# Cumulative sums on 128 partitions and a first q/k pair by heads, in an attention and MLP kernel

## The chip, the cores and the metric

The kernel runs on one core of a Trainium2 chip. A core has five engines that run side by side, each through its own list of instructions in order: TensorE (matrix products), VectorE, ScalarE and GpSimd (work on elements), and SyncE (starts transfers). Sixteen DMA engines move data between the main memory and the on-chip memory SBUF. TensorE writes to a small second memory, PSUM, from which VectorE and ScalarE copy the results. Engines wait for each other through semaphores.

The metric is the device time of one execution in microseconds (us), as the median of several runs. The profiled execution is a run of its own, and its span is a little shorter than its device time, since it counts from the first to the last instruction.

## The reference

Eight batches of eight heads, 576 tokens, head size 64. Each head has q, k, v, and a row s of one number per token.

```python
def attention(q, k, v, s):                       # (8, 8, 576, 64), s: (8, 8, 576)
    scores = (1 / sqrt(64)) * q @ k.T
    cum = cumsum(maximum(s, 0), axis=-1)
    bias = -(cum[:, :, :, None] - cum[:, :, None, :])
    scores = where(causal, -1e9, scores + minimum(bias, 0))
    attn = softmax(scores)                       # over the keys
    return attn @ v

x = attention(...)  # heads side by side: (8, 576, 512)
xn = layernorm(x) * g_ln
out = x + maximum(xn @ w_ch1, 0) @ w_ch2         # 512 -> 2048 -> 512
```

The cumulative sum never falls, so below the diagonal the bias is never positive, and the minimum with 0 changes nothing there. The bias is a term of the query minus a term of the key. The kernel therefore adds it in the scores' own matrix product, by four more rows (64 to 67) beside the 64 of the head size. On the key side they hold the cumulative sum as three bf16 numbers (high, middle and low part, whose sum is nearly exact) and a row of constants; on the query side they hold the high part and constants.

## The kernel before

The kernel is in bf16 after its loads. At its start it does three things at once: it makes the cumulative sums of all 64 heads in float32, it brings q and k of the first heads into the layout that the products need (head size on partitions, tokens along the row), and it loads v. Two heads make a pair. A pair is loaded with six neighbouring tokens to a partition (96 partitions), transposed by TensorE into PSUM, and evacuated from there into the tile kq by VectorE and ScalarE.

```python
QT = 6                      # tokens to a partition
QP = S // QT                # 96 partitions

def ld_pair(kind, g):                            # float32, by SyncE
    tmp = stage.tile([P, 2, QT * D], F32, name="pairtmp", tag="st")
    nc.sync.dma_start(out=tmp[0:QP], in_=pair_src(kind, g))

def ld_cast(kind, g):                            # to bf16 on the way, by GpSimd
    ready[kind, g] = pair_tile(kind)             # from a pool of four buffers
    nc.gpsimd.dma_start(out=ready[kind, g][0:QP], in_=pair_src(kind, g))

def tr_kind(kind, g):                            # six transposes
    ...
    for t in range(QT):
        nc.tensor.transpose(tr[:, t * QP : (t + 1) * QP], src..., ident[0:QP, 0:QP])

def evac_pair(kind, g, engs):                    # two copies, each of both heads
    ...

def keep_warm(n):                                # matmuls on zeros: filler
    for _ in range(n):
        nc.tensor.matmul(w, lhsT=zeros[:, 0:P], rhs=zeros, start=True, stop=True)
```

The start, in the order of the program (every engine takes its own instructions out of it in this order):

```python
nc.sync.dma_start(out=c_in, in_=s.rearrange("b h s -> (b h) s"))    # 64 rows of 576
ld_pair("k", 0)
ld_pair("q", 0)
...                                              # constants are set
keep_warm(12)
...
ld_cast_pair(1); ld_cast_pair(2)
for t in range(NT): ld_cast_v(0, t)              # five tiles of v of batch 0
ld_cast_pair(3); ld_w1(0)
...
nc.vector.tensor_scalar(out=c_in, in0=c_in, ...)                    # relu, times 8
nc.vector.tensor_tensor_scan(out=c_sc, data0=c_one, data1=c_in, ...)   # cumulative sum
cast_pair("k", 0, "act")
cast_pair("q", 0, "act")
nc.vector.tensor_copy(out=c_hi, in_=c_sc)                           # three bf16 parts
nc.vector.tensor_tensor(out=c_in, in0=c_sc, in1=c_hi, op=ALU.subtract)
nc.vector.tensor_copy(out=c_mid, in_=c_in)
nc.vector.tensor_tensor(out=c_lo, in0=c_in, in1=c_mid, op=ALU.subtract)
aug(0, nc.sync, h0=1)         # rows 64 to 67 of heads 1 to 3, SBUF to SBUF by DMA
...
nc.tensor.matmul(ba, lhsT=pick[:, 3, :], rhs=ones[:, 0:512], start=True, stop=False)
tr_kind("k", 0)
keep_warm(2)
tr_kind("q", 0)
nc.tensor.matmul(bq, lhsT=pick[:, 0, :], rhs=c_hi[:, 0:512], ...)   # rows 64 to 67 of head 0
for j, src in enumerate((c_hi, c_mid, c_lo)):
    nc.tensor.matmul(ba, lhsT=pick[:, j, :], rhs=src[:, 0:512], ...)
    ...                                          # one filler between
...                                              # bb: the same for the last 64 tokens
evac_pair("k", 0, ("act", "act"))
nc.scalar.copy(out=kq[0][D : D + 1, 1, 0, 0:512], in_=bq[32:33])
evac_pair("q", 0, ("dve", "act"))
nc.vector.tensor_copy(out=kq[0][D:KA, 0, 0, 0:512], in_=ba[0:4])
nc.vector.tensor_copy(out=kq[0][D:KA, 0, 0, 512:S], in_=bb[0:4, 0:TL])
nc.vector.tensor_copy(out=kq[0][D : D + 1, 1, 0, 512:S], in_=bb[32:33, 0:TL])
keep_warm(5)
```

Then the heads follow, n = 0 to 63. For the first eight:

```python
scores(b, h)                  # sa, sb, sc: products into PSUM; then exp by ScalarE
if h in (1, 3, 5, 6): scores_d(b, h // 2)
if h in (0, 2, 4):            # pairs 1, 2, 3
    qk_pair(h // 2 + 1, ("dve", "dve"), ("act", "dve" if h < 4 else "act"))
...
if n % 2 == 1 or n == 0: keep_warm(2)
if n > 1: pv_next()           # product with v of an earlier head (pot), VectorE divides by the sum
```

After head 8 TensorE also has the two products of the MLP (ph and py) in a queue, and units of that queue fill it up between the heads until the end.

Of the kernel before, what the change touches and what calls it, by code (L numbers as in the profile page):

```python
# [19 lines left out]
def kernel(  # L20
# [11 lines left out]
    nc = tc.nc  # L32
    B, H, S, D = q.shape
# [9 lines left out]
    BH = B * H  # L43
# [7 lines left out]
    NR = 4  # L51
    QT = 6
    QP = S // QT

    const = ctx.enter_context(tc.tile_pool(name="const", bufs=1))
    stage = ctx.enter_context(tc.tile_pool(name="stage", bufs=6))
# [29 lines left out]
    cT = const.tile([P, NT, 2, BH, 4], BF16, name="cT")  # L86
    xm = [const.tile([P, Dm], F32, name=f"xm{i}") for i in range(4)]
    xTm = const.tile([P, KD, 512], BF16, name="xTm")
    c3 = const.tile([BH, 3, S], BF16, name="c3")
    c_hi, c_mid, c_lo = (c3[:, j, :] for j in range(3))  # L90
    zeros = const.tile([P, 512], BF16, name="zeros")
    ones = const.tile([BH, S], BF16, name="ones")
    minus = const.tile([1, S], BF16, name="minus")
# [12 lines left out]
    ready = {}  # L106


    def pair_src(kind, g):
        src = k if kind == "k" else q  # L110
        b, j = g // 4, g % 4
        return src[b, 2 * j : 2 * j + 2].rearrange("h (p t) d -> p h (t d)", t=QT)

    def pair_tile(kind):
        return pairs.tile([P, 2, QT * D], BF16, name=kind + "p", tag=kind + "p")

    def ld_pair(kind, g):
        tmp = stage.tile([P, 2, QT * D], F32, name="pairtmp", tag="st")
        nc.sync.dma_start(out=tmp[0:QP], in_=pair_src(kind, g))
        loaded[kind, g] = tmp  # L120

    def cast_pair(kind, g, eng):
        ready[kind, g] = pair_tile(kind)
        copy_on(eng, ready[kind, g][0:QP], loaded.pop((kind, g))[0:QP])

    def ld_cast(kind, g):
        ready[kind, g] = pair_tile(kind)
        nc.gpsimd.dma_start(out=ready[kind, g][0:QP], in_=pair_src(kind, g))

    def ld_cast_pair(g):  # L130
        ld_cast("k", g)
# [112 lines left out]
        tr_kind("k", g)  # L244
        tr_kind("q", g)

    def tr_kind(kind, g):
        src = ready.pop((kind, g))
        if g < 5:
            tr = ps_m.tile([P, S], BF16, name="trqk", tag="m")  # L250
        else:
            tr = ps_t.tile([P, S], BF16, name="trqk", tag="tr")
        for t in range(QT):

            nc.tensor.transpose(
                tr[:, t * QP : (t + 1) * QP],
                src[0:QP].rearrange("p h c -> p (h c)")[:, t * P : (t + 1) * P],
                ident[0:QP, 0:QP],
            )
        trs[kind, g] = tr  # L260

    def evac_pair(kind, g, engs):
        tr = trs.pop((kind, g))
        hh = (g % 2) * 2
        dst = kq[(g // 2) % 2][0:D, "kq".index(kind), hh : hh + 2, 0:S].rearrange(
            "d u (p r w) -> d u p r w", r=QT // 2, w=2
        )
        for w in range(2):
            copy_on(
                engs[w],  # L270
                dst[:, :, :, :, w],
                tr[w * D : (w + 1) * D, :].rearrange("d (u r p) -> d u p r", u=2, p=QP),
            )

    def qk_pair(g, k_engs, q_engs):
# [289 lines left out]
    def keep_warm(n):  # L565
# [2 lines left out]
            nc.tensor.matmul(w, lhsT=zeros[:, 0:P], rhs=zeros, start=True, stop=True)  # L568


    c_in, c_sc, c_one, warm = (
        yop.tile([P, S], F32, name="c_in", tag="yo")[0:BH],
        yop.tile([P, S], F32, name="c_sc", tag="yo")[0:BH],
        yop.tile([P, S], F32, name="c_one", tag="yo")[0:BH],
        small.tile([P, 2], F32, name="warm", tag="warm", bufs=1),
    )
    nc.sync.dma_start(out=c_in, in_=s.rearrange("b h s -> (b h) s"))
    ld_pair("k", 0)
    ld_pair("q", 0)

    ONE2 = 1.0019378662109375
    NEG2 = -1.0058441162109375
    nc.vector.memset(zeros.bitcast(F32), 0.0)
    nc.vector.memset(warm, 0.0)
    nc.scalar.activation(out=warm[:, 1:2], in_=warm[:, 0:1], func=ACT.Exp)
    keep_warm(12)
    nc.vector.memset(c_one, 1.0)
    nc.vector.memset(pick.rearrange("p j m -> p (j m)").bitcast(F32), 0.0)
    for j in range(3):
# [31 lines left out]
    for t in range(NT):  # L621
        ld_cast_v(0, t)
    ld_cast_pair(3)
    ld_w1(0)
    v_edges(1)
    nc.vector.tensor_scalar(
        out=c_in, in0=c_in, scalar1=0.0, scalar2=1.0 / scale, op0=ALU.max, op1=ALU.mult
    )
    nc.vector.tensor_tensor_scan(
        out=c_sc, data0=c_one, data1=c_in, initial=0.0, op0=ALU.mult, op1=ALU.add  # L630
    )
    cast_pair("k", 0, "act")
    cast_pair("q", 0, "act")
    nc.vector.tensor_copy(out=c_hi, in_=c_sc)
    nc.vector.tensor_tensor(out=c_in, in0=c_sc, in1=c_hi, op=ALU.subtract)
    nc.vector.tensor_copy(out=c_mid, in_=c_in)
    nc.vector.tensor_tensor(out=c_lo, in0=c_in, in1=c_mid, op=ALU.subtract)
    aug(0, nc.sync, h0=1)
    constant_rows(1)
    aug(1, nc.sync)  # L640
# [3 lines left out]
    bb = ps_s.tile([P, 512], F32, name="bb", tag="s")  # L644
    bq = ps_s.tile([P, 512], F32, name="bq", tag="s")
    nc.tensor.matmul(ba, lhsT=pick[:, 3, :], rhs=ones[:, 0:512], start=True, stop=False)
    tr_kind("k", 0)
    keep_warm(2)
    tr_kind("q", 0)
    nc.tensor.matmul(bq, lhsT=pick[:, 0, :], rhs=c_hi[:, 0:512], start=True, stop=True)  # L650
    for j, src in enumerate((c_hi, c_mid, c_lo)):
        nc.tensor.matmul(
# [4 lines left out]
    for j, src in ((3, ones), (0, c_hi), (1, c_mid), (2, c_lo)):  # L657
        nc.tensor.matmul(
            bb[:, 0:TL], lhsT=pick[:, j, :], rhs=src[:, 512:S], start=(j == 3), stop=(j == 2)
        )  # L660
# [213 lines left out]
```

The softmax here doesn't subtract the row's maximum and nothing guards it: scores larger than these inputs give would overflow.

## Time and profile before

| what | value |
|---|---|
| device time, median of 3 runs | 367.0 us (366.61 to 367.05) |
| span of the profiled execution | 366.8 us |
| TensorE busy | 355.0 us, 97% |
| VectorE busy | 202.9 us, 55% |
| ScalarE busy | 191.3 us, 52% |
| GpSimd busy | 164.9 us, 45% |
| moved by DMA | 52.17 MB, 142 GB/s on average |

In the lines of the profile, PE is TensorE, PEld its loading of weights, DVE VectorE, ACT ScalarE, POOL GpSimd and SP SyncE. L12 is line 12 of the kernel. An output and an input are given as `out<-in` by their tiles' names. A busy share is an average over the whole span, and a start of ten or twenty microseconds can look quite different from the rest; so the views that matter here are those that keep the order of time: the chain of waits (followed back from the last instruction, at each step to what released it) and the timelines of single engines. A long start of a matmul after the one in front of it doesn't say by itself what TensorE waited for; the filler matmuls are work too in the profile's eyes.

### The profile page before, as it was taken

How to read it: one execution, taken by the hardware profiler on the slowest of the kernel's cores; microseconds unless marked ns; L12 is line 12 of the kernel's file. 1: busy time of each engine (PE TensorE's matmuls, PEld its weight loads, DVE VectorE, ACT ScalarE, POOL GpSimd, SP SyncE). 2: the span in 40 equal slices, each digit the busy share in tenths (PEclk: the TensorE clock that was granted, in tenths of full speed). 3: DMA queues.
4: the chain of work that ended last, by engine and by line, in shares of the span. 5: the costliest groups of instructions: out<-in, count | busy, mean ns of one | idle time of the engine just before them, and what ended most of it. 6: DMA issues, size and time to landing. Idle time of an engine off the chain costs nothing.

```text
span 366.8 us, 8315 instructions
## 1 busy us (share of the span) xinstructions
PE 355.0 (97%) x3017; PEld 197.1 (54%) x3067; DVE 202.9 (55%) x535; ACT 191.3 (52%) x367; POOL 164.9 (45%) x447
## 2 busy tenths in 40 slices
PE   8998999999999999999999999999999999999995
PEld 3677555565555555555455555555555554444444
DVE  7697789684357554944384547743675483112211
ACT  5895988467732673367534753476337522501410
POOL 8854468667633656344675563554852101000000
PEclk9999999999999999999999999999999999999999
DMA  8999999999965999599979986798830011011013
GB/s 144 162 195 178 202 211 193 163 240 176 183 146 141 206 199 181 104 215 163 188 176 213 194 183 140 189 191 182 174 102 2 0 59 57 1 58 59 0 31 86
DMA packets 156653, 52.17 MB, mean 142 GB/s; under 512 B 143641, under 2 KB 151940, under 8 KB 156612
## 3 DMA queue, kind: packets, MB, share of 16 engines
q1 hardware_dynamic: 138868, 43.08, 55.5%
q0 software_dynamic: 17344, 8.03, 18.9%
q8 instruction: 24, 0.39, 0.5%
q10 hardware_dynamic: 400, 0.52, 0.4%
q14 instruction: 17, 0.14, 0.2%
HBM read 37.11 MB, written 9.44 MB: 127 GB/s over the span
## 4 chain that ended last, share of the span: by engine, by line
PE 72%; DVE 7%; DMA 6%; SPq 4%; POOL 4%; issue 3%; ACT 3%; POOLq 0%; ACTq 0%
PE py L515 26%; PE ph L497 25%; PE pot L389 6%; SPq L164 3%; PE sc L312 3%; PE sa L312 3%; PE sb L312 3%; DMA rowtmp<-in_q_dram 2%; PE idle L568 2%; DMA vtmp<-in_v_dram 2%; DVE xn L451 2%; PE trx L484 2%; DVE stats L423 1%; POOL er L331 1%; ACT er L323 1%
## 5 line engine op out<-in xcount | busy, mean ns | idle before, releaser
L515 PE MATMUL py<-w_bf,hT 128*128 128x512 bf16 (+1 forms) x565 | 132.1, 373 | 1.6 <-DVE yo L524 0.4
L497 PE MATMUL ph<-xT,w_bf 128*128 128x512 bf16 x478 | 116.4, 379 | 1.1 <-DVE yo L524 0.2
L507 ACT ACTIVATE hT<-ph 128x512 bf16<-128x512 f32 x102 | 61.0, 598 | 64.4 <-PE ph L497 64.4
L515 PEld LDWEIGHTS <-hT 128*128 128x128 bf16 x592 | 53.5, 98 | 49.1 <-issue 0.9
L497 PEld LDWEIGHTS <-w_bf 128*128 128x128 bf16 x560 | 50.1, 97 | 51.3 <-issue 2.9
L323 ACT ACTIVATE er<-sa 128x512 bf16<-128x512 f32 x64 | 38.2, 597 | 70.9 <-PE sa L312 50.1
L331 POOL TENSOR_SCALAR_AFFINE_SELECT er<-er 128x128 bf16<-128x128 bf16 x216 | 59.7, 300 | 22.5 <-ACT er L323 22.3
L505 DVE TENSOR_SCALAR hT<-ph 128x512 bf16<-128x512 f32 x38 | 26.3, 692 | 56.7 <-PE ph L497 49.0
L176 POOL CAST rows<-rowtmp 128x512 bf16<-128x512 f32 (+1 forms) x55 | 33.5, 609 | 50.7 <-DMA rowtmp<-in_q_dram 46.0
L312 PEld LDWEIGHTS <-kq 68*128 68x128 bf16 x452 | 33.4, 97 | 27.4 <-issue 1.7
L389 PEld LDWEIGHTS <-er 128*128 128x128 bf16 x960 | 37.5, 98 | 14.9 <-issue 0.7
L389 PE MATMUL pot<-v_bf,er 128*128 128x65 bf16 x960 | 40.2, 193 | 0.5 <-PE sd L355 0.3
L397 DVE RECIPROCAL rinv<-pot 128x5 f32<-128x5 f32 x64 | 12.3, 192 | 49.2 <-PE pot L389 48.9
L323 ACT ACTIVATE er<-sc 128x512 bf16<-128x512 f32 x64 | 39.2, 612 | 0.0
L323 ACT ACTIVATE er<-sb 128x512 bf16<-128x512 f32 x64 | 38.4, 599 | 0.3 <-PE sb L312 0.2
L524 DVE SCALAR_TENSOR_TENSOR yo<-py,rstd,xb 128x512 f32<-128x512 f32 x32 | 23.9, 748 | 26.2 <-PE py L515 19.7
L399 DVE TENSOR_TENSOR xb<-pot,rinv 128x256 f32<-128x256 f32 x64 | 27.2, 425 | 2.2
L102 POOL CAST v_bf<-vtmp 128x512 bf16<-128x512 f32 (+1 forms) x30 | 18.5, 617 | 19.6 <-DMA vtmp<-in_v_dram 19.5
L439 POOL TENSOR_TENSOR rstd<-rstd,mhalf 128x4 f32<-128x4 f32 (+1 forms) x8 | 8.8, 1095 | 38.0 <-DVE rstd L438 37.9
L312 PE MATMUL sc<-kq 68*128 68x256 bf16 (+1 forms) x216 | 25.3, 229 | 0.3
L423 DVE BATCH_NORM_STATS2 stats<-xb 128x6 f32<-128x128 f32 (+2 forms) x100 | 25.3, 313 | 0.4
L312 PE MATMUL sb<-kq 68*128 68x64 bf16 (+1 forms) x172 | 24.5, 244 | 0.9 <-DMA kq<-rows 0.6
(101 smaller groups left out, 322.1 us busy)
## 6 DMA issues: line engine op xcount, KB each, us to landing
out_dram<-yo SPq DMA_DIRECT2D x32, 256.0 KB
vtmp<-in_v_dram SPq DMA_DIRECT2D x24, 256.0 KB
rowtmp<-in_k_dram SPq DMA_DIRECT2D x44, 128.0 KB
rowtmp<-in_q_dram SPq DMA_DIRECT2D x44, 128.0 KB
w_bf<-in_moe_w_ch_dram POOLq DMA_DIRECT2D x8, 512.0 KB, 10.7
kp<-in_k_dram POOLq DMA_DIRECT2D x9, 144.0 KB, 6.8
qp<-in_q_dram POOLq DMA_DIRECT2D x9, 144.0 KB, 7.0
v_bf<-in_v_dram POOLq DMA_DIRECT2D x8, 128.0 KB, 8.1
```

The costliest lines, as they stand in the source:

```text
L176: nc.gpsimd.tensor_copy(out=r[0:pn, :, :, 0:D], in_=loaded.pop(("rows", gam, t))[0:pn])
L312: nc.tensor.matmul(a[:, c + a0 - q0 : c + a1 - q0], lhsT=k_cols(b, h, kb), rhs=cols, start=True, stop=not (pe_mask and diag),)
L323: nc.scalar.activation(out=e[:, o : o + 512], in_=a, func=ACT.Exp, scale=scale)
L331: nc.gpsimd.affine_select(out=e[:, o : o + P], in_=e[:, o : o + P], compare_op=ALU.is_ge, fill=0.0, base=0, pattern=[[1, P]], channel_mult ...
L389: nc.tensor.matmul(pot[:, t, :], lhsT=e[:, o : o + P], rhs=vv[:, kb, h, :], start=(kb == 0), stop=(kb == last),)
L399: nc.vector.tensor_tensor(out=xb[b][:, :, hs], in0=pot[:, 0:NF, 0:D], in1=rinv[:, 0:NF].unsqueeze(2).to_broadcast([P, NF, D]), op=ALU.mult,)
L423: nc.vector.bn_stats(out=st[b][:, t, part, :], in_=x[:, lo:hi])
L497: nc.tensor.matmul(ph, lhsT=w1_bf[:, kd, fb * P : (fb + 1) * P], rhs=xT[:, kd, :], start=(kd == 0), stop=(kd == KD - 1),)
L505: nc.vector.tensor_scalar_max(out=hT[:, fb, :], in0=ph, scalar1=0.0)
L507: nc.scalar.activation(out=hT[:, fb, :], in_=ph, func=ACT.Relu)
L515: nc.tensor.matmul(py[0], lhsT=hT[:, fb, t * P : (t + 1) * P], rhs=w2_bf[:, fb, c0:c1], start=(fb == 0), stop=(fb == FB - 1),)
L524: nc.vector.scalar_tensor_tensor(out=yo, in0=py[0], scalar=rs, in1=x[:, c0:c1], op0=ALU.mult, op1=ALU.add)
```

## The change

The change works on the start alone.

- **Cumulative sums in two halves of tokens.** 64 heads have used 64 of 128 partitions. Now partitions 0 to 63 hold tokens 0 to 319 and partitions 64 to 127 hold tokens 256 to 575. The sum of tokens 0 to 255, which the second half needs as its first value (carry), comes from a ScalarE Relu with a sum. The three bf16 parts are then made for both halves at once, and tokens 320 to 575 are copied back to partitions 0 to 63. It is for a shorter row of VectorE operations.
- **First pair by heads.** k and q of pair 0 are loaded, cast, transposed and evacuated one head at a time, over two issuing engines (SyncE and ScalarE), so that head 0 needn't wait for head 1. Head 1's part comes after the scores of head 0.
- **Twelve tokens to a partition for pairs 1 to 3** (48 partitions), in space of the tiles hT and w2_bf that is not yet used then. Each transfer has half as many, longer rows, and TensorE has twelve transposes of 48 columns instead of six of 96 for each of k and q.
- Fewer filler matmuls: eight at first instead of twelve, and others moved.

```diff
+    HC = 320
-    c3 = const.tile([BH, 3, S], BF16, name="c3")
-    c_hi, c_mid, c_lo = (c3[:, j, :] for j in range(3))
+    c3 = const.tile([P, 3, S], BF16, name="c3")
+    c_hi, c_mid, c_lo = (c3[0:BH, j, :] for j in range(3))
...
+    def qt_of(g):
+        return 2 * QT if 1 <= g <= 3 else QT
...
+    def pair_tile(kind, g):
+        if 1 <= g <= 3:
+            big = hT if g < 3 else w2_bf
+            o = (0, 6, 0)[g - 1] + "kq".index(kind) * 3
+            return big[0 : S // qt_of(g), o : o + 3, :].rearrange(...)
...
+    def ld_head(kind, u, eng):                  # one head, float32
+    def cast_head(kind, u, eng):
...                                              # tr_kind and evac_pair take us=(0,), (1,) or (0, 1)
-    nc.sync.dma_start(out=c_in, in_=s.rearrange("b h s -> (b h) s"))
-    ld_pair("k", 0)
-    ld_pair("q", 0)
+    nc.sync.dma_start(out=c_in[0:BH, 0:HC], in_=s_r[:, 0:HC])
+    nc.scalar.dma_start(out=c_in[BH:P, HC:S], in_=s_r[:, 0 : S - HC])
+    nc.sync.dma_start(out=c_in[BH:P, 0:HC], in_=s_r[:, S - HC : S])
+    ld_head("k", 0, nc.scalar)
+    ld_head("q", 0, nc.sync)
+    ld_head("k", 1, nc.scalar)
+    ld_head("q", 1, nc.sync)
...
-    keep_warm(12)
+    keep_warm(8)
+    nc.vector.memset(carry, 0.0)
...
+    nc.scalar.activation(
+        out=c_sc[BH:P, HC:S], in_=c_in[BH:P, HC:S], func=ACT.Relu,
+        scale=1.0 / scale, accum_out=carry[BH:P],
+    )
+    cs, ci = c_sc[:, 0:HC], c_in[:, 0:HC]
...                                              # the same tensor_scalar and scan on cs and ci,
+    ... initial=carry ...                        # with the carry as the first value
+    def second_half(j):
+        nc.vector.tensor_copy(out=c3[0:BH, j, HC:S], in_=c3[BH:P, j, 2 * HC - S : HC])
-    cast_pair("k", 0, "act")
-    cast_pair("q", 0, "act")
+    cast_head("k", 0, "act")
+    cast_head("q", 0, "act")
...                                              # the three parts, second_half after each
-    tr_kind("k", 0)
-    keep_warm(2)
-    tr_kind("q", 0)
+    tr_kind("k", 0, (0,))
+    keep_warm(1)
+    tr_kind("q", 0, (0,))
+    keep_warm(1)
...
-    evac_pair("k", 0, ("act", "act"))
+    evac_pair("k", 0, ("act", "act"), (0,))
+    evac_pair("q", 0, ("act", "act"), (0,))
     nc.scalar.copy(out=kq[0][D : D + 1, 1, 0, 0:512], in_=bq[32:33])
-    evac_pair("q", 0, ("dve", "act"))
-    nc.vector.tensor_copy(out=kq[0][D:KA, 0, 0, 0:512], in_=ba[0:4])
+    cast_head("k", 1, "dve")
+    nc.vector.tensor_copy(out=kq[0][D:KA, 0, 0, 0:P], in_=ba[0:4, 0:P])
+    nc.vector.tensor_copy(out=kq[0][D:KA, 0, 0, P:512], in_=ba[0:4, P:512])
+    cast_head("q", 1, "act")
...
-    keep_warm(5)
+    tr_kind("k", 0, (1,))
+    keep_warm(2)
...                                              # in head 0 (n == 0), after its scores:
+            if h == 0:
+                tr_kind("q", 0, (1,))
+                evac_pair("k", 0, ("dve", "dve"), (1,))
+                evac_pair("q", 0, ("dve", "act"), (1,))
```

More of the change, by code (lines that the diff above doesn't have):

```diff
@@ L111, in pair_src @@
         b, j = g // 4, g % 4
[L112 to L124, printed above, removed]
+        return src[b, 2 * j : 2 * j + 2].rearrange("h (p t) d -> p h (t d)", t=qt_of(g))
+    def pair_tile(kind, g):
+        if 1 <= g <= 3:
+            big = hT if g < 3 else w2_bf
+            o = (0, 6, 0)[g - 1] + "kq".index(kind) * 3
+            return big[0 : S // qt_of(g), o : o + 3, :].rearrange("p a b -> p (a b)").rearrange(
+                "p (h c) -> p h c", h=2
+            )
+        t = pairs.tile([P, 2, QT * D], BF16, name=kind + "p", tag=kind + "p")
+        return t[0:QP]
+    def ld_head(kind, u, eng):
+        if u == 0:
+            loaded[kind] = stage.tile([P, 2, QT * D], F32, name="pairtmp", tag="st")
+            ready[kind, 0] = pair_tile(kind, 0)
+        eng.dma_start(out=loaded[kind][0:QP, u], in_=pair_src(kind, 0)[:, u])
+    def cast_head(kind, u, eng):
+        copy_on(eng, ready[kind, 0][:, u], loaded[kind][0:QP, u])
     def ld_cast(kind, g):
-        ready[kind, g] = pair_tile(kind)
-        nc.gpsimd.dma_start(out=ready[kind, g][0:QP], in_=pair_src(kind, g))
+        ready[kind, g] = pair_tile(kind, g)
+        nc.gpsimd.dma_start(out=ready[kind, g], in_=pair_src(kind, g))
     def ld_cast_pair(g):
@@ L245, in tr_pair, with tr_kind, evac_pair @@
         tr_kind("q", g)
[L247 to L263, printed above, removed]
-        hh = (g % 2) * 2
-        dst = kq[(g // 2) % 2][0:D, "kq".index(kind), hh : hh + 2, 0:S].rearrange(
-            "d u (p r w) -> d u p r w", r=QT // 2, w=2
+    def tr_kind(kind, g, us=(0, 1)):
+        src = ready[kind, g].rearrange("p h c -> p (h c)")
+        n = qt_of(g) // 2
+        qp = S // qt_of(g)
+        if us[0] == 0:
+            if g < 5:
+                trs[kind, g] = ps_m.tile([P, S], BF16, name="trqk", tag="m")
+            else:
+                trs[kind, g] = ps_t.tile([P, S], BF16, name="trqk", tag="tr")
+        tr = trs[kind, g]
+        for u in us:
+            for t in range(u * n, u * n + n):
+                nc.tensor.transpose(
+                    tr[:, t * qp : (t + 1) * qp],
+                    src[:, t * P : (t + 1) * P],
+                    ident[0:qp, 0:qp],
+                )
+    def evac_pair(kind, g, engs, us=(0, 1)):
+        tr = trs[kind, g]
+        hh = (g % 2) * 2
+        u0, u1 = us[0], us[-1] + 1
+        n = qt_of(g) // 2
+        qp = S // qt_of(g)
+        dst = kq[(g // 2) % 2][0:D, "kq".index(kind), hh + u0 : hh + u1, 0:S].rearrange(
+            "d u (p r w) -> d u p r w", r=n, w=2
         )
@@ L271, in evac_pair @@
                 dst[:, :, :, :, w],
-                tr[w * D : (w + 1) * D, :].rearrange("d (u r p) -> d u p r", u=2, p=QP),
+                tr[w * D : (w + 1) * D, u0 * n * qp : u1 * n * qp].rearrange(
+                    "d (u r p) -> d u p r", r=n, p=qp
+                ),
             )
@@ L568, in keep_warm @@
             nc.tensor.matmul(w, lhsT=zeros[:, 0:P], rhs=zeros, start=True, stop=True)
[L571 to L574, printed above, removed]
+    c_in, c_sc, c_one, warm, carry = (
+        yop.tile([P, S], F32, name="c_in", tag="yo"),
+        yop.tile([P, S], F32, name="c_sc", tag="yo"),
+        yop.tile([P, S], F32, name="c_one", tag="yo"),
         small.tile([P, 2], F32, name="warm", tag="warm", bufs=1),
+        small.tile([P, 1], F32, name="carry", tag="carry", bufs=1),
     )
-    nc.sync.dma_start(out=c_in, in_=s.rearrange("b h s -> (b h) s"))
-    ld_pair("k", 0)
-    ld_pair("q", 0)
+    s_r = s.rearrange("b h s -> (b h) s")
+    nc.sync.dma_start(out=c_in[0:BH, 0:HC], in_=s_r[:, 0:HC])
[5 more added lines that the diff above has]
+    ld_head("q", 1, nc.sync)
     ONE2 = 1.0019378662109375
@@ L625 @@
     v_edges(1)
+    nc.scalar.activation(
+        out=c_sc[BH:P, HC:S],
+        in_=c_in[BH:P, HC:S],
+        func=ACT.Relu,
+        scale=1.0 / scale,
+        accum_out=carry[BH:P],
+    )
+    cs, ci = c_sc[:, 0:HC], c_in[:, 0:HC]
     nc.vector.tensor_scalar(
-        out=c_in, in0=c_in, scalar1=0.0, scalar2=1.0 / scale, op0=ALU.max, op1=ALU.mult
+        out=ci, in0=ci, scalar1=0.0, scalar2=1.0 / scale, op0=ALU.max, op1=ALU.mult
     )
     nc.vector.tensor_tensor_scan(
-        out=c_sc, data0=c_one, data1=c_in, initial=0.0, op0=ALU.mult, op1=ALU.add
+        out=cs, data0=c_one[:, 0:HC], data1=ci, initial=carry, op0=ALU.mult, op1=ALU.add
     )
-    cast_pair("k", 0, "act")
-    cast_pair("q", 0, "act")
[L634 to L637, printed above, removed]
+    def second_half(j):
+        nc.vector.tensor_copy(out=c3[0:BH, j, HC:S], in_=c3[BH:P, j, 2 * HC - S : HC])
+    cast_head("k", 0, "act")
+    cast_head("q", 0, "act")
+    nc.vector.tensor_copy(out=c3[:, 0, 0:HC], in_=cs)
+    second_half(0)
+    nc.vector.tensor_tensor(out=ci, in0=cs, in1=c3[:, 0, 0:HC], op=ALU.subtract)
+    nc.vector.tensor_copy(out=c3[:, 1, 0:HC], in_=ci)
+    second_half(1)
+    nc.vector.tensor_tensor(out=c3[:, 2, 0:HC], in0=ci, in1=c3[:, 1, 0:HC], op=ALU.subtract)
+    second_half(2)
     aug(0, nc.sync, h0=1)
```

## The prediction

> **What bounds the kernel now.** The summary of the page says that TensorE is busy for 97% of the span. That says little about a change in the first 20 us, so I read the chain of waits next, cut to its first 23 us, and then the timeline of each engine there. The chain is TensorE from 1.26 us on, but mostly filler: matmuls on a tile of zeros (L568) whose result nobody uses.
>
> ```profile
> 1.26 5.30 PE idle L568 x12
> 6.57 0.47 PE ba L646
> 7.04 0.36 PE trqk L255 x6
> ...
> 9.59 0.32 PE ba L652
> 9.90 0.12 PE bb L658 x4
> 10.02 1.19 PE idle L568 x5
> 11.21 0.22 PE sa L312
> ```
>
> Columns: start, length, what. Of the 9.95 us between the first filler and the first scores matmul (sa), 5.30 + 0.43 + 0.32 + 0.32 + 1.19 = 7.56 us are filler. So TensorE only looks like the bound; filler covers the wait for others. Who are they? VectorE, first of all (start, length, engine, line, operation, and in brackets the idle time before it and what ended it):
>
> ```profile
> 3.94 0.60 DVE L626 TENSOR_SCALAR c_in<-c_in 64x576 f32<-64x576 f32 x1 [0.81 <-DMA c_in<-in_s_dram]
> 4.58 1.35 DVE L629 TENSOR_TENSOR_SCAN c_sc<-c_one,c_in 64x576 f32<-64x576 f32 x1
> 5.96 0.52 DVE L634 CAST c<-c_sc 64x576 bf16<-64x576 f32 x1
> 6.51 0.75 DVE L635 TENSOR_TENSOR c_in<-c_sc,c 64x576 f32<-64x576 f32 x1
> 7.30 0.45 DVE L636 CAST c<-c_in 64x576 bf16<-64x576 f32 x1
> 7.79 0.75 DVE L637 TENSOR_TENSOR c<-c_in,c 64x576 bf16<-64x576 f32 x1
> ```
>
> The cumulative sum and its three bf16 parts take from 3.94 to 8.54 us, 4.60 us on 64 partitions. Then come the ba matmul and three small copies, the last ending at 10.99 us; sa starts at 11.04. Beside it ScalarE waits 3.3 us for the first k pair until 5.61, then casts, evacuates and copies until 10.48.
>
> Two gates stand after that. Head 1 starts at 13.14 us, when a transfer that the last cumulative part feeds has landed:
>
> ```profile
> 13.14 0.10 PEld L312 LDWEIGHTS <-kq 68*128 68x128 bf16 x1 [0.59 <-DMA kq<-c]
> ```
>
> And the first product with v (pv) starts at 16.18 us. Its fifteenth matmul, the first to read the fifth v tile, stops briefly before 16.77 us. The transfers table gives 6.8 us from issue to landing for that tile and the timeline its issue at 9.95 us, so it landed at about 16.75 us:
>
> ```profile
> 16.34 0.42 PE pot L389 x14
> 16.77 0.00 issue
> 16.77 0.19 PE pot L389
> ```
>
> So there are three gates in a row: first scores, head 1, v. A gain passes only if all three move. From 60 to 360 us TensorE is busy for 296.25 of 300 us, so what is left at 20 us should reach the end.
>
> **What the Trainium skill says.** "VectorE: DVE Perf Modes", section "Side-by-side: where the cycles go": an operation costs some 150 cycles (0.16 us) besides its elements. The trace agrees: 576 elements in a subtract at one per cycle give (576 + 150)/0.96 = 0.756 us, and it shows 0.75. "ScalarE: Activation LUTs", section "What ACT_TABLE_LOAD costs": 1283 ns; here 1.28 us. "DMA: Bandwidth & Descriptors", section "Anatomy of one DMA": about 2 us of fixed cost, most of it completion. Here the s load ends its issue at 1.41 us and releases VectorE at 3.94, 2.5 us later. "TensorE: Matmul & The Clock Gate", Part 1: half clock until a busy window of about 3.4 us has passed. The twelve fillers start 0.43 us apart, the last five 0.22; this run only sped up at about 6.4 us, over 5 us after its first matmul.
>
> **The change, part by part.**
>
> Cumulative sums. The free size goes from 576 to 320 on 128 partitions. Scaling what is above 0.16 us by 320/576: tensor_scalar 0.60 to 0.40, scan 1.35 to 0.82, casts 0.52 and 0.45 to 0.36 and 0.32, the two subtracts 0.75 to 0.49 each. Sum 4.42 to 2.88, saving 1.54 us. Added are three copies of 256 bf16 down to the lower partitions, 0.2 us each as an estimate from that page: 0.6, and 0.1 for their gaps. Net 0.8 us. But the upper half's data is the second transfer on SyncE's queue, issued 0.6 us later, though each is smaller. I let it land 0.3 us later, at 4.2 us. ScalarE gives the carry: three DMA issues at 0.5 us (what its issues at the kernel's end take) from 0.81, the table load of 1.28, then a Relu over 256, about 0.4: ready at about 4.3 us, before the scan starts at 4.65. The last part is then complete at about 8.0 us instead of 8.54: **0.5 us**, not 1.5.
>
> First pair by head. The first k head comes with half the bytes, but behind the s pieces; I leave its landing near 5.4 us. ScalarE then casts two heads (0.83/2 plus fixed cost, about 0.45 each, to 6.3), evacuates four pieces of 288 at 0.43 (to 8.0) and copies the q row, 0.57 (to 8.6). Before it did twice as much and ended at 10.48. VectorE, after 8.0, casts k head 1 (0.4), copies the 128 columns that sa needs (0.26), done at 8.7. TensorE has the transposes of k head 1 and two fillers, to 9.2. So sa starts at about 9.3 us instead of 11.04: **1.7 us** at the first gate. But the second head of the pair now falls behind it: VectorE still has 1.0 us of copies and three of 288 (0.43 each), ScalarE one behind three exps at 0.49 spacing. ScalarE: exp from 9.8, that copy to 11.8. Pair 1's q transposes need the same PSUM buffer, so they come at 11.8 and end at 12.2, then two fillers: head 1 at about 12.7. Its transfer, issued 0.5 us earlier, lands at about 12.6. Second gate: **0.45 us** instead of 1.7.
>
> Fillers. Eight instead of twelve first, 14 instead of 21 in all up to sa: it only lets the rest move up. At 0.43 us, eight end near 4.7, the ba start matmul near 5.1, and TensorE then has a gap until the first transposes at about 5.9.
>
> Twelve tokens. A partition reads 3,072 B instead of 1,536 and there are half as many rows. TensorE gets 24 transposes of 48 columns instead of 12 of 96: twelve took 0.51 us, 0.043 each, and a 65-column matmul takes 0.030 each, so 24 cost at most 0.7. That is 0.1 to 0.2 us per pair, in three places. The evacuations keep their 576 elements. What it is worth lies in the queue: pairs 1 and 2 land at 7.4, 8.1, 9.6 and 10.3 us (issue plus 3.9, 3.8, 4.7, 4.8) and v follows, a tile every 1.1 to 1.5 us. If the 3 us between the first and the last pair load shrink by a sixth, all v tiles come 0.5 us earlier: third gate, **0.5 us**. Pairs 4 and 5 get fresh buffers, which removes a 0.65 us wait of GpSimd at 16.33; nothing on the path uses that.
>
> The sum is the least of the gates: min(1.7, 0.45, 0.5), with up to 0.2 lost to the small transposes and up to 0.3 won where the head start of ScalarE and VectorE lets fillers be cut short. **Between 0.2 and 0.8 us in the middle case**; I take a gain of 0.6 us, 366.4 us.
>
> **Rivals.** (a) v is the only gate and doesn't move: 48 partitions may be no faster to write, and the s loads grow by 82 KB, since some tokens are read twice or three times. Then 366.9 to 367.2. The stop at 16.77 speaks for it. (b) TensorE stays at half clock past 8 us, because the gap at 5.1 us breaks the busy window. Then ba, bb and the fillers cost double and sa comes at about 10, head 1 still near 13: 366.8 to 367.3. The filler that was put there speaks for the danger; the filler left in each gap speaks against it. (c) Larger descriptors speed the queue up more than I think, and the transfer that feeds head 1 with it, since it waited 3.8 us after its issue among v's packets. Then both late gates move by 1 us and more: 365.3 to 366.0. (d) The extra copies put VectorE on the path in pairs 1 to 3; it idles 1.28 and 1.42 us before the evacuations of pairs 1 and 2, so I give this little.
>
> **Range and chances.** (a) and (b) together perhaps 35%, (c) 25%, the middle case 40%. The three times before lie 0.44 us apart. Range 365.3 to 367.3 us. A change of 2% would be 7.3 us, of which nothing in the first 20 us offers even half: faster 0.01, same 0.98, slower 0.01.
>
> **What would show it.** The last cumulative part complete near 8.0 us; carry not what the scan waits for; sa near 9.3; head 1 near 12.7, behind a transfer or the q transposes of pair 1; the first pv not before 15.7, with the fifth v tile landing near 16.2. It is wrong if v's landing hasn't moved, if fillers show 0.43 us spacing after 7 us, or if the later stages take back or add to what stood at 20 us.

## The result: 2.65% slower

The changed kernel takes 376.5 us (median of six; 375.11 to 378.18) beside 366.85 us for the kernel before. The ratio is 1.0265, with a 95% interval of 1.0239 to 1.0291. Some 9.6 us are lost by a change that touches only the first 20 us.

**Where they are lost.** I set the same events of the two traces side by side (us from the start of the span):

| event | before | after | later by |
|---|---|---|---|
| first scores matmul (sa of head 0) | 11.04 | 11.77 | 0.7 |
| sa of head 1 | 13.14 | 17.99 | 4.85 |
| first product with v | 16.18 | 23.62 | 7.4 |
| first transpose of normalised rows (trx) | 31.65 | 40.78 | 9.1 |
| end of the span | 366.8 | 374.8 | 8.0 |

By 41 us everything is lost. (The profiled execution of the kernel before took 368.5 us, 1.7 more than its median. At least part of that lies behind trx: from there to the end it needs 335.2 us, the changed kernel 334.0, and every run below except e17 between 333.6 and 334.6. So the last row is smaller than the difference of the medians.) There are two steps: nearly 5 us at head 1, and over 4 us more between head 1 and trx, 18.5 us before and 22.8 now.

The chain of waits of the changed kernel, cut to the first step (start, length, what):

```profile
8.75 0.03 issue
8.78 0.50 DVE c L681
9.30 0.32 DVE c L672
9.63 0.03 issue
9.65 8.20 DMA kq<-c
17.85 0.14 issue
17.99 0.58 PE sa L334
```

The low part of the cumulative sums is complete at 9.62 us, where it was 8.54. Then the transfer of its rows to heads 1 to 3 takes 8.2 us from the start of its issue; before it was 4.5 (8.67 to 13.1). The timeline of VectorE shows how the low part became late:

```profile
5.03 0.33 DVE L664 TENSOR_SCALAR c_in<-c_in 128x320 f32<-128x320 f32 x1 [1.88 <-DMA c_in<-in_s_dram]
5.46 0.88 DVE L667 TENSOR_TENSOR_SCAN c_sc<-c_one,carry,c_in 128x320 f32<-128x320 f32 x1
6.38 0.71 DVE L676 CAST c<-c_sc 128x320 bf16<-128x320 f32 x1
7.12 0.22 DVE L672 COPY c<-c 64x256 bf16<-64x256 bf16 x1
7.37 0.49 DVE L678 TENSOR_TENSOR c_in<-c_sc,c 128x320 f32<-128x320 f32 x1
7.90 0.33 DVE L679 CAST c<-c_in 128x320 bf16<-128x320 f32 x1
8.26 0.48 DVE L672 COPY c<-c 64x256 bf16<-64x256 bf16 x1
8.78 0.49 DVE L681 TENSOR_TENSOR c<-c_in,c 128x320 bf16<-128x320 f32 x1
9.30 0.32 DVE L672 COPY c<-c 64x256 bf16<-64x256 bf16 x1
```

The scan and the subtracts did get as short as foretold. But s is there 1.1 us later (5.03 instead of 3.94), beside more and smaller loads; one cast takes 0.71 us where its twin takes 0.33, and the copies 0.22 to 0.48. The nine operations take 4.59 us, the six before took 4.60.

The rows are not the whole of the first step. Head 1's scores come behind the transposes of pair 1, and those were late as well, behind ScalarE's copy of head 1's q:

```profile
15.07 0.64 PE L273 MATMUL trqk<-ident,hT 48*128 48x48 bf16 x12 [0.55 <-ACT kq L100]
```

The prediction had them at 11.8 us. With the two fillers behind them TensorE was busy until 16.67 us, so only the last 1.3 of the 4.85 us are a wait for the rows alone.

The second step is TensorE's clock. Two filler matmuls of 512 columns, in the timeline of TensorE of the changed kernel:

```profile
15.64 1.03 PE L590 MATMUL idle<-zeros 128*128 128x512 bf16 x2
17.99 0.58 PE L334 MATMUL sa<-kq 68*128 68x512 bf16 x1 [1.32 <-DMA kq<-c]
19.88 1.04 PE L590 MATMUL idle<-zeros 128*128 128x512 bf16 x2
```

and of the kernel before:

```profile
14.17 0.59 PE L568 MATMUL idle<-zeros 128*128 128x512 bf16 x2
```

Two matmuls end 1.04 us after the first one's start where it was 0.59: they start 0.43 us apart and not 0.22. TensorE runs at half clock, from its first matmul to about 27 us, so part of the first step is paid at half rate too. The column of the granted clock says 1.00 all the while; only the spacing shows it.

### The profile page after: what moved, and what is told of

The parts are those of the page before. It is cut to its first block, busy times and chain, and to the rows that moved or that the text cites. A ratio compares the mean times of both kernels' runs of the same rounds, so it can differ in the third digit from the quotient of the medians.

```text
span 374.8 us, 8454 instructions
## 1 busy us (share of the span) xinstructions
PE 364.2 (97%) x3096; PEld 200.2 (53%) x3096; DVE 203.8 (54%) x543; ACT 192.6 (51%) x372; POOL 164.6 (44%) x447
## 4 chain that ended last, share of the span: by engine, by line
PE 85%; DVE 8%; DMA 3%; ACT 1%; issue 1%; SPq 0%; DVEq 0%
PE py L537 32%; PE ph L519 31%; PE pot L411 7%; PE sc L334 3%; PE sa L334 3%; PE sb L334 3%; DMA kq<-c 2%; PE trx L506 2%; DVE stats L445 1%; DVE xn L473 1%; DVE xb L421 1%; DMA c_in<-in_s_dram 1%; DVE kq L102 1%; PE ph L836 1%; PE trqk L273 1%
## 5 line engine op out<-in xcount | busy, mean ns | idle before, releaser
L537 PE MATMUL py<-w_bf,hT 128*128 128x512 bf16 (+1 forms) x592 | 136.4, 373 | 0.7 <-DVE yo L546 0.7
L519 PE MATMUL ph<-xT,w_bf 128*128 128x512 bf16 x496 | 117.6, 379 | 0.0
L334 PEld LDWEIGHTS <-kq 68*128 68x128 bf16 x452 | 34.4, 100 | 29.6 <-issue 6.5
L334 PE MATMUL sc<-kq 68*128 68x256 bf16 (+1 forms) x216 | 26.4, 235 | 0.3
L334 PE MATMUL sa<-kq 68*128 68x512 bf16 x64 | 25.3, 396 | 1.3 <-DMA kq<-c 1.3
L334 PE MATMUL sb<-kq 68*128 68x64 bf16 (+1 forms) x172 | 25.4, 250 | 0.3 <-ACT hT L851 0.2
## 6 DMA issues: line engine op xcount, KB each, us to landing
w_bf<-in_moe_w_ch_dram POOLq DMA_DIRECT2D x8, 512.0 KB, 10.2
```

The costliest lines, as they stand in the source:

```text
L334: nc.tensor.matmul(a[:, c + a0 - q0 : c + a1 - q0], lhsT=k_cols(b, h, kb), rhs=cols, start=True, stop=not (pe_mask and diag),)
L519: nc.tensor.matmul(ph, lhsT=w1_bf[:, kd, fb * P : (fb + 1) * P], rhs=xT[:, kd, :], start=(kd == 0), stop=(kd == KD - 1),)
L537: nc.tensor.matmul(py[0], lhsT=hT[:, fb, t * P : (t + 1) * P], rhs=w2_bf[:, fb, c0:c1], start=(fb == 0), stop=(fb == FB - 1),)
```

## The experiments

Theory Q held that the loads of 48 partitions clog the transfers, theory C that TensorE's clock is the loss, because fillers were taken away. The first four runs undo or do one part each. Of all runs the ratio to the kernel before (same chip) is given:

| run | what | median us | ratio (95% interval) |
|---|---|---|---|
| e1_six_tokens | after, six tokens again | 372.7 | 1.0154 (1.0113 to 1.0194) |
| e2_before_twelve | before, twelve tokens alone | 368.1 | 1.0018 (0.9996 to 1.0039) |
| e4_twelve_fillers | after, twelve first fillers | 375.5 | 1.0222 (1.0200 to 1.0245) |
| e5_before_eight | before, eight first fillers | 369.1 | 1.0052 (1.0032 to 1.0072) |
| e6_old_sums | after, sums as before | 373.0 | 1.0179 (1.0130 to 1.0228) |
| e7_before_new_sums | before, new sums alone | 368.2 | 1.0048 (1.0027 to 1.0068) |
| e8_before_late_low | before, low part delayed | 370.3 | 1.0088 (1.0061 to 1.0116) |
| e9_no_first_v | after, no loads of batch 0's v | 376.7 | 1.0252 (1.0191 to 1.0314) |
| e10_filled | after, fillers in the gaps | 371.3 | 1.0101 (1.0070 to 1.0132) |
| e12_first_pair_whole | before, new sums and twelve tokens | 375.0 | 1.0202 (1.0161 to 1.0243) |
| e13_heads_alone | before, first pair by heads alone | 371.1 | 1.0084 (1.0046 to 1.0121) |
| e14_heads_filled | the same with fillers | 369.4 | 1.0051 (1.0026 to 1.0075) |
| e15_v_held | e4, v issued after the rows | 372.6 | 1.0163 (1.0095 to 1.0231) |
| e16_v_held_filled | e15 with fillers | 370.8 | 1.0101 (1.0083 to 1.0119) |
| e17_before_no_fillers | before, no filler at all | 371.8 | 1.0124 (1.0098 to 1.0149) |
| e18_late_low_filled | e8 with fillers | 369.6 | 1.0064 (1.0017 to 1.0111) |
| e19_before_rows_of_head | before, twelve tokens on 96 partitions | 367.2 | 0.9986 (0.9971 to 1.0002) |
| e20_whole_filled | e12 with fillers | 369.6 | 1.0051 (1.0030 to 1.0072) |

### One part at a time

```diff
# e1, in the changed kernel (the tile then has 96 partitions)
-        return 2 * QT if 1 <= g <= 3 else QT
+        return QT
```

> The changed kernel with pairs 1 to 3 back at six tokens to a partition (96 partitions, rows of 1,536 B), still in the space of hT and w2_bf. Theory Q (the 48-partition loads clog the transfer queue, so that the rows for head 1 and the v tiles land late): head 1 starts near 13.3 us instead of 17.99, the fifth v tile lands near 17 us instead of 20. Theory C (TensorE stays at half clock because eight fillers are too short a busy stretch): with the same fillers the matmuls of heads 1 to 3 keep their 0.43 us spacing. Q alone: about 367 us. Q and C each for its own part: about 371 to 372 us (4.8 us of the 9.6 gone). C alone: 376 us.

372.7 us: of 9.6 us, some 4 are gone. Head 1 starts at 16.42 us and not near 13.3, and TensorE, which reached full clock by 5.3 us, is back at half clock at 9.0.

```diff
# e2, in the kernel before: qt_of, pair_tile, tr_kind and evac_pair as in the change
+        return 2 * QT if 1 <= g <= 3 else QT
```

> The kernel before with the twelve tokens to a partition alone (48 partitions for pairs 1 to 3, same space as in the changed kernel). Theory Q: head 1 starts at 16.5 to 18 us instead of 13.14 and the fifth v tile lands near 20 instead of 16.75; about 371 us, and up to 375 if TensorE falls back to half clock during the wait. Theory C: nothing but the transposes changes, 367 us.

368.1 us, not told from no change. Head 1 starts at 12.66 us, and the fifth v tile lands 6.5 us after its issue, at 16.1 us (before: 6.8, at 16.75). So the loads of 48 partitions don't clog anything by themselves: theory Q falls as it stood.

```diff
# e4, in the changed kernel; e5 is the same line the other way, in the kernel before
-    keep_warm(8)
+    keep_warm(12)
```

> The changed kernel with twelve fillers at first instead of eight, nothing else. Theory C: the spacing of 512-column matmuls falls to 0.22 us by about 7 us, and the heads after the wait for head 1's rows run at 2.2 us per head pair less; about 372 us. If the wait of some 4 us before head 1 lets the clock fall again, less is won: 374 to 376 us. Theory Q alone: within 0.5 us of the changed kernel, 376 us.

> The kernel before with eight fillers at first instead of twelve, nothing else. Theory C: TensorE keeps 0.43 us spacing to 15 us or beyond, and the first eight heads take some 4 us longer; about 371 us. Theory Q alone: 366.5 to 367 us, since the fillers only cover waits.

Twelve first fillers win 1 us only, eight lose 1.7. In e5's trace, which is of its fastest execution (367.7 us), the clock is at full rate by 6 us all the same, and head 1's rows end its wait at 13.54. So the length of the first stretch is worth 1 to 2 us and is not the loss, and theory C falls in this form. But e4 shows the clock at work. Its stretches (each engine's busy time, then the granted clock, the DMA share and GB/s):

```profile
core 0: us, PE busy (x) PEld busy (x) DVE busy (x) ACT busy (x) POOL busy (x), PEclk, DMA share, GB/s
...
12.00:14.00 2.00, 1.09 (x29) 0.86 (x26) 1.83 (x4) 1.43 (x4) 1.91 (x6) 1.00 3.10 146
14.00:16.00 2.00, 0.34 (x1) 0.00 (x0) 1.33 (x2) 0.64 (x1) 1.10 (x2) 1.00 1.45 106
16.00:18.00 2.00, 1.84 (x13) 1.24 (x14) 0.00 (x0) 1.12 (x2) 1.81 (x3) 0.54 1.28 193
18.00:22.00 4.00, 4.00 (x44) 2.50 (x42) 0.58 (x1) 2.60 (x7) 2.11 (x3) 0.50 1.24 233
22.00:26.00 4.00, 3.72 (x37) 2.54 (x36) 2.52 (x6) 2.59 (x5) 2.38 (x5) 0.50 1.46 194
```

TensorE is busy for 1.09 and 0.34 of 2 us while it waits, first for copies of pair 0 and from 14.3 us on for head 1's rows; right after that its clock is 0.5 and stays there to 26 us. Here the clock column shows it, in a run whose clock had been full before. In the changed kernel it had not been, and the column stayed at 1.00.

### Late low part, or first pair by heads?

Theory L: the low part is late, so its rows meet the packets of v. Theory H: the first pair by heads costs most. The edits put the sums of before into the changed kernel (e6), the new sums into the kernel before (e7), or two idle fills in front of the low part:

```diff
# e8, in the kernel before
+    nc.vector.memset(c_one, 1.0)
+    nc.vector.memset(c_one, 1.0)
     nc.vector.tensor_tensor(out=c_lo, in0=c_in, in1=c_mid, op=ALU.subtract)
```

> The changed kernel with the cumulative sums as before (64 partitions, one load of s, no carry, no copies between partitions); head-by-head first pair, twelve tokens and eight fillers stay. Theory L (the last cumulative part is complete about 1 us later, 9.6 instead of 8.5 us, so its rows for heads 1 to 3 are issued when the v tiles already fill the DMA engines, land 4 to 5 us later, and TensorE falls to half clock while it waits): low part complete near 8.6 us, head 1 starts near 13.5 us, about 368 us. Theory H (splitting the first pair by heads, with its two issuing engines and fewer fillers, is what costs): head 1 still after 16 us, 372 to 376 us.

> The kernel before with the cumulative sums in two halves of tokens alone (three loads of s, carry, copies between partitions); first pair whole, six tokens, twelve fillers. Theory L: low part complete at 9.3 us or later, the rows for head 1 land at 16 us or later, 371 to 376 us. Theory H: low part a little earlier or later by less than 0.5 us, 366.5 to 367.5 us.

> The kernel before with two fills of a 576-element tile (0.54 us each) put in front of the operation that makes the low part: a pure delay of 1.1 us, nothing else changed. Theory L: the delay grows on its way through the DMA engines, rows for head 1 land 3 to 5 us later (16 to 18 us), 371 to 376 us. If the delay just passes through: head 1 near 14.2 us, 368 us.

e6: 373.0 us. Head 1 starts at 15.38, though not behind its rows: pair 1's transposes wait for ScalarE's copy of head 1's q, and the fillers after them run at half clock. That speaks for H; the same wait stands in the changed kernel, at 15.07 us. e7: 368.2 us. Alone, the new sums have the low part complete at 8.30 us, near the 8.0 of the prediction, and yet head 1 starts at 13.77. e8: a delay of 0.9 us moves head 1 by 1.1 us in the profiled execution, so the delay passes through and isn't multiplied there. But its eighteen executions lie between 367.9 and 373.2 us, and the longer ones have the lower mean clock (0.989 to 0.995). L isn't shown by e7 and e8.

```diff
# e9, in the changed kernel; batch 0 then has a constant in place of v
-    for t in range(NT):
-        ld_cast_v(0, t)
+    nc.gpsimd.memset(v_bf[0][:, 0:NF, :, 0:D], 0.5)
+    nc.gpsimd.memset(v_bf[0][0:TL, NF, :, 0:D], 0.5)
```

> The changed kernel without the loads of batch 0's v tiles: GpSimd fills those tiles with a constant instead (so the output of batch 0 is not the reference's). Theory L: with the v packets gone the rows for head 1 land about 2.5 us after their issue, near 12.8 us, TensorE has no long wait; 366 to 369 us, even with eight fillers. Theory H, or a lasting half clock from too few fillers: still 372 us or more.

376.7 us. The time tells nothing on the question, since my edit brought a delay of its own. The timeline of VectorE in e9:

```profile
5.24 3.13 DVE L664 TENSOR_SCALAR c_in<-c_in 128x320 f32<-128x320 f32 x1 [2.10 <-DMA c_in<-in_s_dram]
8.48 0.88 DVE L667 TENSOR_TENSOR_SCAN c_sc<-c_one,carry,c_in 128x320 f32<-128x320 f32 x1
```

and of GpSimd:

```profile
5.89 1.83 POOL L650 MEMSET v_bf<- 128x2048 bf16 x1
7.63 0.55 POOL L651 MEMSET v_bf<- 64x512 bf16 x1
```

An operation that takes 0.33 us elsewhere takes 3.13, and ends soon after the second fill of GpSimd. The Trainium skill, "SBUF — State Buffer", section "SBUF: two separate sides", says that GpSimd and VectorE's faster modes share a port pair, and that one blocks the other for the whole instruction. The trace fits it, but for the first 0.65 us (5.24 to 5.89), in which GpSimd was still issuing loads.

On the question itself the trace does say something. In e9's chain of waits the rows take 6.15 us from the start of their issue, although none of batch 0's v is loaded (GpSimd issues pairs 3 to 5 and weights in its place, and v of batch 1 from 14.2 us on):

```profile
12.29 6.15 DMA kq<-c
```

Theory L expected 2.5 us. So the packets of batch 0's v can't be the only thing that makes the rows late.

### The clock, tested by itself

```diff
# e10, in the changed kernel (e14: the same with 8, in e13; e18 and e20: 8, in e8 and e12)
-    keep_warm(8)
+    keep_warm(12)
...
-                keep_warm(2)
+                keep_warm(12 if n == 0 else 2)
```

> The changed kernel with twelve fillers at first instead of eight and twelve instead of two in front of head 1, so that TensorE has no long gap while it waits for head 1's rows; nothing else. Theory C' (the waits open gaps in TensorE's work, its clock falls to half, and everything up to about 27 us is paid at half rate): matmuls keep 0.22 us spacing from 7 us on, head 1 still starts at 16 to 17 us, and from there to the first transposes of the normalised rows it takes 18.5 us as before instead of 23; about 370.5 us. If the half clock doesn't matter because ScalarE and VectorE set the pace of the heads anyway: 375 us or more.

371.3 us, 5.2 us less than the changed kernel, by added work whose result nobody uses. Head 1 still starts at 16.26 us, and from there to trx it takes 18.8 us as before. Two fillers in e10's timeline of TensorE:

```profile
17.29 0.59 PE L590 MATMUL idle<-zeros 128*128 128x512 bf16 x2
```

So the second step of the loss is the clock, and it is shown. The kernel before needs its fillers as well:

> The kernel before without any filler matmul. Theory C' (fillers hold the clock, and a start at half clock costs what the changed kernel lost): TensorE at half clock to 20 us or later, the first eight heads 4 to 6 us longer; 371 to 374 us. If fillers only fill and the clock recovers by itself within a few us: 365.5 to 367.5 us.

371.8 us: without fillers the kernel before loses 5 us. Its first heads run at half clock until after 19 us, and trx comes at 33.86 us, 2.2 later. The rest is lost behind that: the seven fillers in front of trx are gone as well, and from 35 to 40 us the clock is 0.50 again.

Which part opens the gaps?

> The changed kernel with the first pair whole again and the fillers of before (so: the kernel before with the new cumulative sums and the twelve tokens). The two parts alone cost 0.7 and 1.4 us in their own runs. Theory H' (the head-by-head first pair with its fewer fillers costs most, since it breaks TensorE's busy stretch and lets pair 1 wait for head 1): 367.5 to 369.5 us. If the parts hurt only together, late rows and slow loads: 371 us or more.

> The head-by-head first pair alone, with its eight and further fillers as in the changed kernel; cumulative sums as before, six tokens. Theory H': half clock again from about 9 us to 20 us, head 1 near 15 us though its rows landed by 13.5; 371 to 373 us. If the parts hurt only together: 367 to 368 us.

> The head-by-head first pair alone, as in the run with the sums as before and six tokens, but with twelve fillers at first and eight instead of two in front of head 1. Theory C': full clock from about 7 us on, head 1 near 13.5 us, 366.5 to 368 us, 4 us less than without them. If the order of pair 1 behind head 1's second copies is what costs and not the clock: 370 us or more.

e13: 371.1 us. Its clock falls at about 14 us and not at 9, and its rows land at 14.9 us, 5.7 after the start of their issue, though the sums are those of before. With the fillers of e14 it takes 369.4 us, more than the 366.5 to 368 expected (in e14's profiled execution, the longest with 371.1 us, the clock still fell; in the others its mean is 0.998 or more). e12 missed: 375.0 us, with the first pair whole, where its two parts alone had cost 0.7 and 1.4. In its profile the clock falls to 0.5 at about 16 us. One run was to tell whether that is the clock or the transfers:

> The kernel before with the new cumulative sums and the twelve tokens together (375.0 us, though each part alone costs 0.7 and 1.4), now with eight fillers instead of two in front of head 1. Theory C' (the two parts together open a gap in TensorE's work that is just long enough for its clock to fall, and the clock is the difference): 368.5 to 370 us, all executions close together. If the two parts clog the transfers together: still above 372 us.

369.6 us: 5.4 us come back through six more fillers. So the parts add up where the clock mostly holds: 0.7 (twelve tokens), 1.4 (new sums) and 2.1 (first pair by heads, filled) make 4.2 us, and the whole change with fillers is at 371.3 - 367.3 = 4.0, each of these known to about 1 us. What doesn't add up is the clock: it falls or holds.

The profiled executions also show one thing that the new sums do to the transfers. The loads of pairs 1 and 2 take 4.1 to 4.9 us from issue to landing in the ten kernels that load s in one piece, and 4.8 to 6.5 us in nine of the ten that load it in three (e15 below has 4.5 to 4.6). So three pieces go with slower transfers; why isn't shown.

> The kernel before with the low part made 1.1 us later, and eight fillers instead of two in front of head 1. Without these fillers the times lay between 367.9 and 373.2 us, those with a mean clock of 0.99 the longer ones. Theory C' (the spread is the clock, which falls in some executions during the wait of 1.8 us): all times within 367.5 to 369.5 us. If the spread comes from the transfers: still up to 373 us.

With fillers the clock of all executions is at 0.998 or more, and none exceeds 370.8 us; but they still spread over 2.6 us, from 368.2. The clock explains the long executions of e8, not all of their spread.

### The rows among the packets of v

The first step, head 1's rows, was still open. In e15 GpSimd copies two columns of the low part before it issues v, pair 3 and the first weights, so these come after the rows:

```diff
# e15, in e4 (the same calls are taken out further up); e16 has six fillers in front of head 1 as well
     aug(0, nc.sync, h0=1)
+    nc.gpsimd.tensor_copy(out=held[0:BH], in_=c_lo[:, S - 2 : S])
+    for t in range(NT):
+        ld_cast_v(0, t)
+    ld_cast_pair(3)
+    ld_w1(0)
+    v_edges(1)
```

> The changed kernel with twelve first fillers, and GpSimd held back by one small copy of the low part before it issues the v tiles, pair 3 and the first weights: these transfers are issued some 3.5 us later, behind the rows for head 1. In the run with twelve first fillers alone those rows ended the wait for head 1 at 16.16 us, 5.8 us after their issue, and TensorE then fell to half clock. Theory V (the rows share the DMA engines with the packets of v and wait among them): the rows land 2 to 3 us after their issue, head 1 starts at 13 to 14.5 us, the clock holds; 368 to 371 us unless the later v then becomes the gate. Theory W (the rows are slow by themselves, or for another load): head 1 still at 16 us, 374 to 376 us.

> As the run with v held back, and six fillers instead of two in front of head 1. Theory V: 368 to 369.5 us, the clock surely held. Theory W: 371 to 372 us, as the filled kernel without the hold (371.3).

The wait for the rows is gone, as theory V has it; the time is not as it has it. Head 1 starts at 13.41 us in e15, straight behind the fillers, 2.75 us earlier than in e4. So the rows landed within 4.3 us of the start of their issue (9.13 us), where e4 has 6.4; whether within the 2 to 3 us expected isn't seen. And 0.8 of the 2.75 us come from VectorE. While GpSimd issues no loads, the casts and copies of the sums stay short, and the low part is complete at 8.81 us instead of 9.59. Two lines of e15's VectorE, for which e4 has 0.70 and 0.48 us:

```profile
6.31 0.33 DVE L671 CAST c<-c_sc 128x320 bf16<-128x320 f32 x1
7.81 0.22 DVE L667 COPY c<-c 64x256 bf16<-64x256 bf16 x1
```

But then v is late. TensorE's timeline in e15:

```profile
13.41 0.38 PE L334 MATMUL sa<-kq 68*128 68x512 bf16 x1
...
17.81 0.31 PE L411 MATMUL pot<-v_bf,er 128*128 128x65 bf16 x5 [0.72 <-DMA v_bf<-in_v_dram]
18.54 0.38 PE L334 MATMUL sa<-kq 68*128 68x512 bf16 x1
```

Head 3 starts at 18.54 us where it was 16.80 before, and the clock falls during this wait instead. (Two of e15's four executions take 370.6 us, the other two, with a mean clock of 0.98, take 374.6 and 375.8.) With fillers (e16) the kernel takes 370.8 us: nearly all that the rows won, v gave back (e10: 371.3). In these runs the start is limited by the transfers; the hold only chooses who waits. It moved pair 3 and the weights too, so which of the three the rows had waited among is not told apart, and e9 had late rows without any of this v.

### A version that might win

```diff
# e19, in the kernel before, pairs 1 to 3
+            return two.rearrange("h (p t) d -> (h p) (t d)", t=2 * QT)
```

> The kernel before with twelve tokens to a partition in pairs 1 to 3 in another way: each head takes 48 of the 96 partitions, so a transfer has rows of 3,072 B over 96 partitions, and TensorE keeps six transposes of 96 columns. If the row length helps the queue and the 24 small transposes were what gave the gain back: v lands 0.3 us earlier, 366.6 to 367.2 us, at or just under the kernel before. If the third gate isn't moved by row length: within 0.3 us of before.

367.2 us beside 367.4: the interval (0.9971 to 1.0002) still holds 1. Long rows over all 96 partitions do no harm, and that they gain is not shown.

## Why the prediction was wrong

- **Fillers: "it only lets the rest move up."** This step failed, and more than half of the miss hangs on it. I read 7.56 us of filler as padding, since it covered waits of others. It does a job: it keeps the clock up. Without any, the kernel before loses 5 us (e17); with more in the gaps, the changed kernel wins 5.2 of the 9.6 (e10). Putting back only the four first fillers wins 1 us (e4): what costs is that the waits in front of head 1, which the change made longer, have too little in them.
- **Rival (b), half clock.** I had the mechanism and not its size. I let it last to 8 us or so and cost a few tenths. It lasted to 27 us, and 22.8 instead of 18.5 us passed between head 1 and trx. That a gap later on brings it back I didn't think of, although the fillers between the heads say so.
- **Second gate, "0.45 us".** Foretold were the low part at 8.0 us and its rows at about 12.6. Measured: 9.62 and 17.85. The sum of the VectorE operations was nearly right for the sums alone (8.30 in e7). Beside the head-by-head loads s came at 5.03 us where I had said 4.2, and casts and copies took up to twice their length while GpSimd issued loads (in e15, where it didn't, they kept it). The rows then took 8.2 us for which I had carried over 4.6. The other condition for head 1, pair 1's transposes, was put at 11.8 us and came at 15.07. And the rows were not alone at this gate in the kernel before: in its chain of waits ScalarE's third exponential of head 0 ends at 13.10 us, 0.04 before head 1 starts, which I hadn't read.
- **Third gate, "0.5 us".** No gain is shown. In e2, which is that step alone, the fifth tile lands at 16.1 us, as foretold, but with six tokens it lands anywhere between 15.8 (e8) and 17.1 us (e7), and the time gains nothing. In the changed kernel that tile took 10.2 us from issue to landing, but the first product with v came later still.
- **First gate, "1.7 us".** sa came at 11.77 us, at half clock; with twelve first fillers at 10.64 (e4). That is 0.4 us earlier than in the kernel before, but e2, with the sums and the first pair of before, has it at 10.52. So not even this gain is shown.
- **"The sum is the least of the gates."** Right as a rule: what the first gate does decides nothing. Wrong as a sum, because it had no term for a gate that moves back, and none for the clock, which turns a wait into a longer one.

**Open:** the kernel with all its gaps filled is still 4.0 us above the kernel before. Of these, 3.1 us are there at head 1 (16.26 us in e10 against 13.14) and 3.4 at trx; but head 1 follows straight on the added fillers in e10, so how much of that is the rows can't be read from it. Why the same transfers take 8.2 us in the changed kernel, 6.4 in e4 and 4.5 before, beyond their meeting the loads that GpSimd issued and the slower transfers where s comes in three pieces, wasn't found.

## What to carry to other kernels

Matmuls that compute nothing may be what holds TensorE's clock: before you take them out, ask what the engine does in their place, and look at the spacing of equal matmuls rather than at the clock column. A start that three transfers gate in turn can be limited by the transfers themselves: here a reordering that helped one of them came out of another (e15, e16). Test the parts alone and together: here 0.7 and 1.4 us alone were 7.7 together, and 2.2 once the clock was held.

## What the runs showed of the hardware

- The clock falls during shorter waits than I had thought: in e4 after 4 us in which TensorE was busy for 1.43 us in all. "TensorE: Matmul & The Clock Gate" of the Trainium skill, in "Why this matters for your kernels", warns of gaps over some 3 us; in e4 the one wait for the rows was 1.8 us, beside shorter ones. In e5 the clock held although TensorE was busy for only 0.68 of the 2 us from 12 to 14 us.
- The recorded clock reads 1.00 where TensorE has been at half clock from its first matmul on: 0.43 us spacing up to 26 us in the changed kernel. In e17 both cases stand in one trace: 1.00 up to 30 us, though the matmuls are at half clock until after 19, and 0.50 from 35 to 40 us, after a stretch at full clock.
- A VectorE operation of 0.33 us took 3.13 us while GpSimd issued loads for 0.65 us and then made fills of 1.83 and 0.55 us (e9).
- Casts and copies of VectorE that took 0.70 and 0.48 us while GpSimd issued loads (e4) took 0.33 and 0.22 while it issued none (e15).
